# Gated linear attention, then two MLPs: half-chunk score blocks, a state in mid-chunk and four quadrant tiles

## The chip, the cores and the metric

The kernel runs on one core of a Trainium2 chip. The metric is the device time of one execution in microseconds (us); the profile's "span" is the time from the first to the last instruction of the program.

## The reference, cut to what matters

Attention runs over 4 batches, 8 heads, 768 steps, with heads of 48. Its result goes through two MLPs, as 3072 tokens of width 384.

```python
for t in range(S):
    state = alpha[:, :, t, :, None] * state + np.einsum('bhd,bhe->bhde', k[:, :, t], v[:, :, t])
    y[:, :, t] = np.einsum('bhd,bhde->bhe', q[:, :, t], state)
...
h = x @ w_in                               # 384 -> 2048
x = (h * (1.0 / (1.0 + np.exp(-h)))) @ w_out
gate = 1.0 / (1.0 + np.exp(-(x @ w_gate)))     # 384 -> 1536
return (gate * (x @ w_val) @ w_out2)
```

## The kernel before, in words

**Attention in chunks.** The steps are cut into 24 chunks of 128, six to a batch. Heads go in four pairs, one head of a pair on partitions 0 to 47, the other on 64 to 111. For a chunk c, `prep` (L278) runs the decays as two scans on DVE, multiplies the keys by G (DVE) and the queries by A (POOL in the lead, DVE later). `scores` (L310) transposes the keys on TensorE (L319; four, none for a batch's last chunk) and makes keys times queries (L323, 8 matmuls of 48 x 128 by 128 columns). `scores_done` (L331) multiplies the 2 x 4 x 128 columns by the causal mask on DVE (L334), copies the transposed keys out on ACT (L337) and has ACT square both decay tiles (`check`, L273). `results` (L341) adds to one PSUM bank y: masked scores times values (L352, 8 matmuls of 128 columns), and the state times the queries (L373, 8 of 128 columns); between these it makes the chunk's outer products u (L368, 8 matmuls of 48 columns), to which in the lead an identity matmul adds the old state (L364). `state` (L382) makes the next state from u: in the lead one DVE multiply (L389), later an add (L388) and a multiply. A matmul of float32 operands stands in the trace as two records, each with its own weight load.

**Output of attention.** `y_out` (L399) copies y from PSUM into x and x3 on ACT (L406, L407). After each second chunk six DMAs (L412) move rows of x3 into x; x3 has one buffer, x two. `x_out` (L414) splits x into high and low parts (ACT L422, DVE L423), which are the MLP's input.

**Order.** The first LEAD = 9 chunks run before the MLP (loop at L722): in each round `scores` of c+1, the state of the chunk before, `prep` of c+2, `scores_done`, `x_out`, `results` of c, the loads for c+4 and c+5 (SP queue), and from round 3 on one `bit` (L525) of the conversion of the MLP's weights. Weights come as 64-bit floats and are made into a high and a low part by ACT, DVE and POOL; four bits make one pair of weight tiles. Chunks 9 to 23 run inside the first MLP (loop at L796): each item (b, f) is nine matmuls into a hidden tile h (`mm_in`, L575), its activation (`act`, L581), and nine matmuls out (`mm_out`, L598), all of 512 columns through `mm3` (L562). SCORES and RESULTS (L47 to L53) give the items at which a chunk's `scores` and `results` are put into TensorE's program order, so that each chunk interrupts the MLP's matmuls twice; the `prep` of a chunk is put 3 and 2 items ahead of its scores. Up to item 28 each `act` also does half a weight conversion (`half`, L543), from a count `n_half` that the lead leaves behind.

**PSUM.** Of eight banks two are the pool ps_h (h in turn, in the lead also the transposed keys t and u), and two groups of three hold two_banks (scores, later s) and bank (y).

Of the kernel before, what the change touches and what calls it, by code (L numbers as in the profile page):

```python
# [17 lines left out]
P = 128  # L18
# [13 lines left out]
QW = 3 * NP * C  # L32
N = 512
# [17 lines left out]
for _c in range(13, NC):  # L51
    SCORES[_c] = (_c // 4 - 1, (0, 4, 8, 11)[_c % 4], 0)
    RESULTS[_c] = (_c // 4 - 1, (2, 6, 10, 13)[_c % 4], 0)  # L53

# [127 lines left out]
def gated_attention_then_mlps(ctx: ExitStack, tc: tile.TileContext, qka, a0, v, w_in, w_out, w_gate, w_val, w_out2, out):  # L182
# [25 lines left out]
    causal = ap.tile([P, C], F32, name="causal")  # L208

    W = ap.tile([DP, NP * D + 16], F32, name="state")  # L210
    W_all = W[:, : NP * D].rearrange("r (p d) -> r p d", d=D)
# [31 lines left out]
    def constants():  # L243
# [5 lines left out]
        nc.gpsimd.affine_select(out=causal, in_=causal, compare_op=ALU.is_ge, fill=0.0, base=0, pattern=[[1, C]], channel_multiplier=-1)  # L249
# [5 lines left out]
        nc.gpsimd.memset(W, 0.0)  # L255
# [17 lines left out]
    def check(c, i):  # L273

        x = (Gt, At)[i].pop(c)
        nc.scalar.activation(x, x, AF.Square, accum_out=chk[:DP, c, i : i + 1])

    def prep(c, step, p0=0, p1=NP, mul=None):  # L278
# [5 lines left out]
        if step == 0:  # L284
            if p0 == 0:
                Gt[c] = G_at[c % 2]
                At[c] = ap.tile([DP, NP * C], F32, tag="A", name="A", bufs=2)
# [11 lines left out]
        elif step == 1:  # L299
            nc.vector.tensor_tensor_scan(At[c][:, lo:hi], t[:, A_OFF + lo : A_OFF + hi], d1[:, lo:hi], 0.0, op0=ALU.mult, op1=ALU.add)  # L300
        else:
            q = t[:, lo:hi]
            mul.tensor_tensor(q, q, At[c][:, lo:hi], op=ALU.mult)

    S, T, M, KT, U, Y = {}, {}, {}, {}, {}, {}

# [3 lines left out]
    def scores(c, g, apart, p0=0, p1=NP):  # L310

        t = qk[c]
        if p0 == 0:
            S[c] = two_banks(g)
            if not last_of(c):
                T[c] = ps_h.tile([P, N], F32, tag="h", name="t") if apart else bank(g)
        for p in range(p0, p1):
            if not last_of(c):
                nc.tensor.transpose(T[c][:, p * DP : (p + 1) * DP], t[:, NP * C + p * C : NP * C + (p + 1) * C], ident)  # L319
        for p in range(p0, p1):  # L320
            for j in range(2):
                r = 64 * j
                nc.tensor.matmul(  # L323
                    S[c][:, j, p * C : (p + 1) * C],
                    t[r : r + D, NP * C + p * C : NP * C + (p + 1) * C],
                    t[r : r + D, p * C : (p + 1) * C],
                    start=True,
                    stop=True,
                )

    def scores_done(c):  # L331
        for_all = causal.rearrange("s (j i t) -> s j i t", j=1, i=1).to_broadcast([P, 2, NP, C])
        M[c] = ap.tile([P, 2, NP, C], F32, tag="m", name="m", bufs=2)
        nc.vector.tensor_tensor(M[c], S[c].rearrange("s j (i t) -> s j i t", i=NP), for_all, op=ALU.mult)  # L334
        if not last_of(c):
            KT[c] = ap.tile([P, NP, DP], F32, tag="kt", name="kt", bufs=2)
            nc.scalar.activation(KT[c], T.pop(c)[:, : NP * DP].rearrange("t (p d) -> t p d", p=NP), AF.Copy)  # L337
        check(c, 0)
        check(c, 1)

    def results(c, g):  # L341


        y = Y[c] = bank(g)
        first = c % CB == 0

        v_c = vt[c].rearrange("t h e -> t (h e)")
        for p in range(NP):
            for j, n in ((0, 64), (1, D)):
                r, h = 64 * j, (2 * p + j) * D  # L350

                nc.tensor.matmul(  # L352
                    y[r : r + n, p * C : (p + 1) * C], v_c[:, h : h + n], M[c][:, j, p], start=p == 0, stop=first, skip_group_check=True
                )
        s = S.pop(c)
        if not last_of(c):
            u = ps_h.tile([P, N], F32, tag="h", name="u")[:DP] if c < LEAD else s[:DP, 0]
            U[c] = u[:, : NP * D]
            kt = KT.pop(c)
            sums = c < LEAD and not first  # L360
            if sums:
                for j, n in ((0, 64), (1, D)):
                    r = 64 * j
                    nc.tensor.matmul(u[r : r + n, : NP * D], ident[r : r + D, r : r + n], W[r : r + D, : NP * D], start=True, stop=False, skip_group_check=True)  # L364
            for p in range(NP):
                for j, n in ((0, 64), (1, D)):
                    r = 64 * j
                    nc.tensor.matmul(u[r : r + n, p * D : (p + 1) * D], kt[:, p, r : r + n], vt[c][:, 2 * p + j], start=not sums, stop=True, skip_group_check=True)  # L368
        if not first:
            for p in range(NP):  # L370
                for j, n in ((0, 64), (1, D)):
# [527 lines left out]
```

## Time and profile before

| what | value |
|---|---|
| median of 3 runs | 975.56 us (974.47 to 976.59) |
| profiled execution, its own time | 976.87 us |
| its span | 974.8 us |
| mean granted TensorE clock | 0.987 |
| PE, DVE, ACT, POOL busy | 951.3, 450.6, 381.9, 92.9 us |

The program's instructions are listed by line and engine. "PE" is a matmul, "PEld" a weight load, which overlaps matmuls. A duration of a matmul includes its way through the array, so that several overlap; how fast matmuls follow one another is read from their starts.

### The profile page before, as it was taken

What the parts mean: (1) busy time and instruction counts of PE and PEld (TensorE: products, weight loads), DVE (VectorE), ACT (ScalarE), POOL (GpSimd) and SP (SyncE); (2) the same over time, 40 slices, a digit from 0 to 9 for tenths busy, and PEclk for the clock granted to TensorE, in tenths of its full rate; (3) what the DMA queues carried; (4) which work ended last, traced back from release to release, by engine and by line L of the source; (5) the groups of instructions that cost most, each with busy time, mean ns of one, the idle gap of its engine ahead of it and who ended that gap; (6) DMA issues with size and microseconds to landing.
All of it is one profiled execution on the core that took longest, in us unless ns stands there. A gap on an engine that the chain in (4) does not pass through costs nothing.

```text
span 974.8 us, 12868 instructions
## 1 busy us (share of the span) xinstructions
PE 951.3 (98%) x5192; PEld 777.2 (80%) x5192; DVE 450.6 (46%) x640; ACT 381.9 (39%) x707; POOL 92.9 (10%) x105
## 2 busy tenths in 40 slices
PE   7879999999999999999999999999999999999997
PEld 5658887878888888888888888888888888888885
DVE  8777778644543434342766444443232222222221
ACT  3446666443334334333666344433222222221211
POOL 2223323100000000000221111110000000000000
PEclk8899999999999999999999999999999999999999
DMA  9753332130111210003332112001000000000001
GB/s 229 210 150 117 129 100 80 40 107 28 58 42 37 70 38 13 5 1 102 98 98 67 63 65 65 33 1 42 24 1 0 33 1 1 33 1 0 33 1 37
DMA packets 35348, 54.84 MB, mean 56 GB/s; under 512 B 3856, under 2 KB 24368, under 8 KB 35280
## 3 DMA queue, kind: packets, MB, share of 16 engines
q1 hardware_dynamic: 34512, 53.37, 17.9%
q8 instruction: 43, 0.70, 0.3%
q10 hardware_dynamic: 768, 0.56, 0.2%
q14 instruction: 25, 0.20, 0.1%
HBM read 48.02 MB, written 4.72 MB: 54 GB/s over the span
## 4 chain that ended last, share of the span: by engine, by line
PE 89%; DVE 3%; DMA 2%; ACT 2%; issue 1%; POOL 1%; SPq 0%; ACTq 0%; DVEq 0%
PE h L565 13%; PE h L567 13%; PE h L566 13%; PE s L565 6%; PE s L567 5%; PE s L566 5%; PE o L567 3%; PE o L565 3%; PE o L566 3%; PE v L565 3%; PE v L566 3%; PE v L567 3%; PE y L565 3%; PE y L567 3%; PE y L566 3%; PE s L323 2%
## 5 line engine op out<-in xcount | busy, mean ns | idle before, releaser
L565 PE MATMUL h<-x,w 128*128 128x512 f32 x582 | 228.0, 392 | 3.1 <-ACT w L504 1.7
L567 PE MATMUL h<-x,w 128*128 128x512 f32 x582 | 227.0, 390 | 0.8 <-POOL w L522 0.8
L566 PE MATMUL h<-x,w 128*128 128x512 f32 x582 | 227.0, 390 | 0.0
L593 DVE TENSOR_TENSOR gl<-g,gh 128x512 fp32r<-128x512 f32 x168 | 115.9, 690 | 194.9 <-ACT gh L592 194.2
L592 ACT ACTIVATE gh<-g 128x512 fp32r<-128x512 f32 x168 | 106.2, 632 | 157.0 <-DVE g L587 153.9
L565 PEld LDWEIGHTS h<-x,w 128*128 128x128 f32 x582 | 109.2, 188 | 28.0 <-ACT w L504 2.1
L567 PEld LDWEIGHTS h<-x,w 128*128 128x128 f32 x582 | 109.3, 188 | 25.0 <-POOL w L522 1.7
L566 PEld LDWEIGHTS h<-x,w 128*128 128x128 f32 x582 | 109.2, 188 | 22.8
L584 ACT ACTIVATE g<-h 128x512 f32<-128x512 f32 x96 | 57.0, 593 | 154.8 <-PE h L567 154.8
L587 DVE TENSOR_TENSOR g<-v,g 128x512 f32<-128x512 f32 x46 | 31.8, 692 | 178.7 <-PE v L567 178.7
L565 PE MATMUL s<-gl,w 128*128 128x512 f32 x240 | 96.5, 402 | 0.0
L586 ACT ACTIVATE g<-h 128x512 f32<-128x512 f32 x72 | 42.9, 596 | 132.6 <-PE h L567 132.6
L567 PE MATMUL s<-gh,w 128*128 128x512 f32 x240 | 93.7, 390 | 0.0
L566 PE MATMUL s<-gh,w 128*128 128x512 f32 x240 | 93.6, 390 | 0.0
L565 PE MATMUL o<-gl,w 128*128 128x512 f32 x144 | 56.1, 390 | 0.0
L567 PE MATMUL o<-gh,w 128*128 128x512 f32 x144 | 56.1, 390 | 0.0
L566 PE MATMUL o<-gh,w 128*128 128x512 f32 x144 | 56.1, 389 | 0.0
L522 POOL TENSOR_TENSOR w<-tmp,w 128x384 fp32r<-128x384 f32 x36 | 36.4, 1030 | 195.0 <-ACT w L504 195.0
L565 PEld LDWEIGHTS s<-gl,w 128*128 128x128 f32 x240 | 45.0, 187 | 12.4 <-issue 1.4
L587 DVE TENSOR_TENSOR g<-h,g 128x512 f32<-128x512 f32 x26 | 18.0, 692 | 79.3 <-PE h L567 79.3
L565 PE MATMUL v<-x,w 128*128 128x512 f32 x138 | 53.9, 391 | 0.0
L566 PE MATMUL v<-x,w 128*128 128x512 f32 x138 | 53.8, 390 | 0.0
(120 smaller groups left out, 1280.8 us busy)
## 6 DMA issues: line engine op xcount, KB each, us to landing
x<-in_moe_w_in SPq DMA_DIRECT2D x16, 384.0 KB, 3.6
x<-in_moe_w_out SPq DMA_DIRECT2D x16, 384.0 KB, 4.1
x<-in_qka SPq DMA_DIRECT2D x12, 448.0 KB, 4.2
qk<-in_qka SPq DMA_DIRECT2D x11, 448.0 KB, 3.7
v<-in_v SPq DMA_DIRECT2D x24, 192.0 KB, 3.1
raw<-in_moe_w_gate SPq DMA_DIRECT2D x12, 384.0 KB, 3.5
raw<-in_moe_w_val SPq DMA_DIRECT2D x12, 384.0 KB, 3.8
raw<-in_moe_w_out SPq DMA_DIRECT2D x12, 384.0 KB, 3.7
```

The source lines that it names most:

```text
L323: nc.tensor.matmul(S[c][:, j, p * C : (p + 1) * C], t[r : r + D, NP * C + p * C : NP * C + (p + 1) * C], t[r : r + D, p * C : (p + 1) * C] ...
L522: nc.gpsimd.tensor_tensor(l, b[:, i * SW : (i + 1) * SW].bitcast(F32), h.bitcast(F32), op=ALU.subtract)
L565: nc.tensor.matmul(ps, wh, x_l, start=first, stop=False)
L566: nc.tensor.matmul(ps, wh, x_h, start=False, stop=False)
L567: nc.tensor.matmul(ps, wl, x_h, start=False, stop=last)
L584: nc.scalar.activation(g, h, AF.Silu)
L586: nc.scalar.activation(g, h, AF.Sigmoid)
L587: nc.vector.tensor_tensor(g, val, g, op=ALU.mult)
L592: nc.scalar.activation(gh, g, AF.Copy)
L593: nc.vector.tensor_tensor(gl, g, gh.bitcast(F32), op=ALU.subtract)
```

## The change

Each chunk is seen as two halves of 64 steps. Scores are made only inside each half (two diagonal blocks of 64 x 64), and what the second half gets from the first comes through a state taken at mid-chunk. Matmuls of scores, sums (u, now one per half), values and queries become 64 columns wide (sums 48) and lie in the four quadrants of the array; there are 16 of each where there were 8. Keys are transposed for every chunk. W becomes two tiles of two states each. A drain of TensorE stands before the queries. In the MLP there is one visit per chunk: transposes of c+2, sums of c+1, values of c, scores of c+1, queries of c. In the lead the old state is added to u by one identity matmul (`carry`), only for the first half. x3 is gone (x has the fourth block of rows itself), the six DMAs of a pair of chunks go to SP, only those of chunk 7 to both queues. The lead no longer prepares chunk 9; it does 8 conversion bits and one more ACT step in place of 6 bits. The preparations of chunks 9 to 13 have items of their own.

```diff
-CONV = {c: 1 for c in range(3, LEAD)}
+CONV = {c: 1 for c in range(3, LEAD - 1)}
-SCORES = {9: (1, 12, 0), 10: (1, 13, 0), 11: (1, 14, 0), 12: (1, 15, 2)}
-RESULTS = {9: (1, 12, 1), 10: (1, 13, 1), 11: (1, 14, 1), 12: (2, 2, 0)}
-DECAYS = {10: ((1, 9), (1, 10)), 11: ((1, 12), (1, 12)), 12: ((1, 14), (1, 14))}
+FIRST = {"T": (1, 11, 0), "scores": (1, 12, 0)}
+VISIT = {9: (1, 12, 1), 10: (1, 13, 1), 11: (1, 14, 1)}
+G_AT = {9: (1, 5), 10: (1, 7), 11: (1, 9), 12: (1, 11), 13: (1, 13)}
+A_AT = {9: (1, 6), 10: (1, 8), 11: (1, 10), 12: (1, 12)}
+for _c in range(12, NC):
+    VISIT[_c] = (_c // 4 - 1, (2, 6, 10, 13)[_c % 4], 0)
...
+    def scores(c, p0=0, p1=NP):
+        t = qk[c]
+        if p0 == 0:
+            S[c] = bank(0), bank(1) if c < LEAD else ps_h.tile([P, N], F32, tag="h", name="s")
         for p in range(p0, p1):
-            for j in range(2):
-                r = 64 * j
+            for h in range(2):
+                for j in range(2):
+                    r, o = 64 * j, p * C + h * HC
+                    nc.tensor.matmul(
+                        S[c][j][h * HC : (h + 1) * HC, p * HC : (p + 1) * HC],
+                        t[r : r + D, K_OFF + o : K_OFF + o + HC],
+                        t[r : r + D, o : o + HC],
...
     def scores_done(c):
+        for j, s in enumerate(S.pop(c)):
+            nc.vector.tensor_tensor(M[c][:, j], s[:, :UA].rearrange("s (i t) -> s i t", i=NP), for_all, op=ALU.mult)
...
+    def sums(c):
+        for p in range(NP):
+            for h in range(2):
+                for j, n in ((0, 64), (1, D)):
+                    r, o = 64 * j, UA + p * D
+                    if h == 0 or not last_of(c + 1):
+                        nc.tensor.matmul(
+                            yu[r : r + n, h, o : o + D],
+                            kt[h * HC : (h + 1) * HC, p, r : r + n],
+                            vt[c + 1][h * HC : (h + 1) * HC, 2 * p + j],
...
+    def queries(c):
+        nc.tensor.drain()
+        for p in range(NP):
+            for h in range(1 if first_of(c) else 0, 2):
+                for j in range(2):
+                    r, to, n = 64 * j, 64 * (j ^ h), D if h or j else 64
+                    nc.tensor.matmul(
+                        yu[to : to + n, h, p * HC : (p + 1) * HC],
+                        w[r : r + D, h, p * D : p * D + n],
+                        qk[c][r : r + D, p * C + h * HC : p * C + (h + 1) * HC],
...
     def state(c):
+        u = [YU[c - 1][0][:DP, h, UA : UA + NP * D] for h in range(2)]
+        wa, wb = (W[c % 2][:, h, : NP * D] for h in range(2))
+        if c < LEAD:
+            nc.scalar.activation(wb, u[0], AF.Copy)
+        elif first_of(c):
+            nc.vector.tensor_copy(wb, u[0])
         else:
-            nc.vector.tensor_tensor(w, u, w, op=ALU.add)
+            nc.vector.tensor_tensor(wb, u[0], wa, op=ALU.add)
+        if not last_of(c):
+            nc.vector.tensor_tensor(W[(c + 1) % 2][:, 0, : NP * D], u[1], wb, op=ALU.add)
+            if c + 1 in AE:
+                decay(c + 1)
...
+        nc.scalar.activation(x[:DP, :, o, :HC], yu[:DP, 0], AF.Copy)
+        for j in range(2):
+            r, at = 64 * j, 64 * (1 - j)
+            nc.scalar.activation(x[r : r + D, :, o, HC:], yu[at : at + D, 1], AF.Copy)
...
+        def visit(c):
+            open_results(c, 0)
+            if c + 2 < NC:
+                keys(c + 2)
+            if c + 1 < NC:
+                sums(c)
+            values(c)
+            if c + 1 < NC:
+                scores(c + 1)
+                queries(c)
+
+        def visited(c):
+            if c + 5 < NC and c != LEAD - 1:
+                load_decays(c + 5)
...
+            if c == LEAD - 1:
+                for _ in range(3):
+                    way1.bit()
+                way1.a_scalar(2)
+                way1.n_half = 3
+                x_out(c - 1)
```

## Rows read from the trace of the kernel before

**Rows 1.** Page: busy time of each engine; the chain that ended last.

```profile
PE 951.3 (98%) x5192; PEld 777.2 (80%) x5192; DVE 450.6 (46%) x640; ACT 381.9 (39%) x707; POOL 92.9 (10%) x105
...
PE 89%; DVE 3%; DMA 2%; ACT 2%; issue 1%; POOL 1%; SPq 0%; ACTq 0%; DVEq 0%
```

**Rows 2.** Stretches: busy us of PE, PEld, DVE, ACT, POOL; clock, DMA share, GB/s.

```profile
0.00:61.00 61.00, 49.03 (x536) 37.72 (x538) 50.85 (x76) 25.08 (x69) 15.89 (x26) 0.83 0.80 214
61.00:74.00 13.00, 9.05 (x79) 6.23 (x76) 6.46 (x11) 7.09 (x14) 1.31 (x2) 1.00 0.43 129
...
120.00:180.00 60.00, 59.22 (x258) 47.84 (x257) 45.57 (x60) 37.59 (x63) 18.91 (x18) 1.00 0.24 81
```

**Rows 3.** Timeline of PE, one chunk's two visits: start, length (us), line, tiles.

```profile
183.42 0.55 PE L319 MATMUL y<-ident,qk 112*128 112x112 f32 x4
183.90 1.16 PE L323 MATMUL s<-qk 48*128 48x128 f32 x16
184.99 0.50 PE L565 MATMUL s<-gl,w 128*128 128x512 f32 x1
...
186.94 0.40 PE L567 MATMUL y<-gh,w 128*128 128x512 f32 x1
187.27 1.09 PE L352 MATMUL y<-m,v 128*64 128x128 f32 x16
188.18 0.62 PE L368 MATMUL s<-v,kt 128*48 128x48 f32 x16
188.73 1.08 PE L373 MATMUL y<-qk,state 48*64 48x128 f32 x16
189.75 0.50 PE L565 MATMUL h<-x,w 128*128 128x512 f32 x1
```

**Rows 4.** Timeline of PE where only the MLP runs: eleven matmuls, first and last.

```profile
301.74 0.39 PE L566 MATMUL y<-gh,w 128*128 128x512 f32 x1
...
304.00 0.39 PE L567 MATMUL h<-x,w 128*128 128x512 f32 x1
```

**Rows 5.** Groups of PE by form, 304.3 to 306.8 us: busy us, mean ns.

```profile
L352 PE MATMUL y<-m,v 128*64 128x128 f32 x8 | 1.1, 279 | 0.0
...
L368 PE MATMUL s<-v,kt 128*64 128x48 f32 x8 | 0.6, 220 | 0.0
```

**Rows 6.** Timeline of the lead: PE, the transposes of two rounds that follow each other.

```profile
23.02 0.60 PE L319 MATMUL t<-ident,x 112*128 112x112 f32 x4
...
27.74 0.60 PE L319 MATMUL t<-ident,qk 112*128 112x112 f32 x4
```

**Rows 7.** Groups of DVE by form, 6.9 to 61.3 us: busy, mean ns | idle before.

```profile
L334 DVE TENSOR_TENSOR m<-s,causal 128x1024 f32<-128x1024 f32 x9 | 10.8, 1197 | 0.0
...
L423 DVE TENSOR_TENSOR x<-x,x 128x768 fp32r<-128x768 f32 x3 | 3.1, 1028 | 3.5 <-ACT x L422 3.5
L389 DVE TENSOR_TENSOR state<-u,aend 112x192 f32<-112x192 f32 x6 | 2.1, 353 | 1.3 <-PE u L368 0.8 <-POOL x L303 0.3 <-PE y L373 0.2
...
L298 DVE TENSOR_TENSOR qk<-qk,G 112x256 f32<-112x256 f32 x1 | 0.4, 426 | 0.2 <-DMA qk<-in_qka 0.2
```

**Rows 8.** Timeline of DVE late in the lead: three of chunk 9's five preparation steps.

```profile
56.63 1.22 DVE L298 TENSOR_TENSOR qk<-qk,G 112x512 f32<-112x512 f32 x1
57.77 1.21 DVE L300 TENSOR_TENSOR_SCAN A<-qk,d 112x512 f32<-112x512 f32 x1
59.02 0.69 DVE L303 TENSOR_TENSOR qk<-qk,A 112x512 f32<-112x512 f32 x1
```

**Rows 9.** Groups of ACT, 24 to 76 us: the first copy of y_out.

```profile
L406 ACT ACTIVATE x<-y 112x128 f32<-112x128 f32 x7 | 1.9, 278 | 15.4 <-PE y L373 10.0 <-DMA x<-x 5.3
```

**Rows 10.** Waits of PE, longest first: us in total, times, longest.

```profile
PE u L364 <- DVE state L389: 4.8, 2, 4.0
...
PE h L565 <- ACT w L504: 1.7, 1, 1.7
```

**Rows 11.** Line L412, its DMAs on SP: duration ns min/median/max.

```profile
L412 SPq DMA_DIRECT2D x<-x x60: 507/587/1459, 28.9 to 449.1; - x60
```

More of the change, by code (lines that the diff above doesn't have):

```diff
@@ L32 @@
 QW = 3 * NP * C
+HC = C // 2
+UA = NP * HC
 N = 512
@@ L303, in prep, with first_of, open_keys, keys @@
             mul.tensor_tensor(q, q, At[c][:, lo:hi], op=ALU.mult)
-    S, T, M, KT, U, Y = {}, {}, {}, {}, {}, {}
+    S, T, M, KT, YU = {}, {}, {}, {}, {}
     def last_of(c):
         return c % CB == CB - 1
-    def scores(c, g, apart, p0=0, p1=NP):
+    def first_of(c):
+        return c % CB == 0
+    def open_keys(c):
+        T[c] = ps_h.tile([P, N], F32, tag="h", name="t")
+    def keys(c, p0=0, p1=NP):
+        t = qk[c]
+        if c not in T:
+            open_keys(c)
+        for p in range(p0, p1):
+            nc.tensor.transpose(T[c][:, p * DP : (p + 1) * DP], t[:, K_OFF + p * C : K_OFF + (p + 1) * C], ident)
@@ L347, in results, with values @@
+    def values(c):
+        yu, _ = YU[c]
         v_c = vt[c].rearrange("t h e -> t (h e)")
         for p in range(NP):
[L349 to L368, printed above, removed]
@@ L692, in gated_attention_then_mlps @@
         way1.load(0)
-        late = []
-        def states():
-            while late and (last_of(late[0]) or late[0] + 1 in AE):
-                c = late.pop(0)
-                if not last_of(c):
-                    state(c)
-        def results_done(c):
-            late.append(c)
-            if c >= LEAD - 1:
-                states()
+        def visit(c):
[11 more added lines that the diff above has]
+                load_decays(c + 5)
             if c + 4 < NC:
@@ L708, in results_done @@
                 load_values(c + 4)
+        for p0, p1 in ((0, 2), (2, NP)):
+            for s in range(3):
+                prep(0, s, p0, p1, nc.vector)
+            keys(0, p0, p1)
+            scores(0, p0, p1)
+        load_decays(4)
+        keys_done(0)
+        prep(1, 0)
+        keys(1)
+        open_results(-1, 1)
+        sums(-1)
+        scores_done(0)
+        keys_done(1)
+        prep(1, 1)
+        prep(1, 2)
+        state(0)
+        YU.pop(-1)
+        prep(2, 0)
+        early = {}
+        for c in range(LEAD):
+            open_results(c, c % 2)
+            if c + 1 < LEAD:
+                sums(c)
+            values(c)
+            if c + 1 < LEAD:
+                scores(c + 1)
+            else:
+                early[0, 0] = mm_in(ps_h, "h", "in", 0, 0)
+            queries(c)
+            if c + 1 < LEAD:
+                carry(c + 1)
+            if c + 2 < LEAD:
+                keys(c + 2)
+            if c + 2 < LEAD:
+                prep(c + 2, 1)
+                prep(c + 2, 2)
+            if c + 3 < LEAD:
+                prep(c + 3, 0)
+            if c + 1 < LEAD:
+                scores_done(c + 1)
+                state(c + 1)
+            if c + 2 < LEAD:
+                keys_done(c + 2)
+            if c == LEAD - 1:
[4 more added lines that the diff above has]
+                x_out(c - 1)
+            visited(c)
             y_out(c)
@@ L750, in put @@
                 todo.setdefault((i, place), []).append((what, c))
-            for c, (b, f, end) in SCORES.items():
-                put(at[b, f], end, "scores", c)
-                if c > LEAD:
-                    first, then = (at[x] for x in DECAYS[c]) if c in DECAYS else (at[b, f] - 3, at[b, f] - 2)
-                    put(first, 3, "prep0", c)
-                    put(then, 3, "prep1", c)
-            for c, (b, f, end) in RESULTS.items():
-                put(at[b, f], end, "results", c)
-                put(at[b, f] + 1, 1, "x_out", c)
+            b, f, end = FIRST["T"]
+            put(at[b, f], end, "keys", LEAD)
+            b, f, end = FIRST["scores"]
+            put(at[b, f], end, "keys", LEAD + 1)
+            put(at[b, f], end, "first", LEAD)
+            for c, x in G_AT.items():
+                put(at[x], 3, "G", c)
+            for c, x in A_AT.items():
+                put(at[x], 3, "A", c)
+            for c, (b, f, end) in VISIT.items():
+                i = at[b, f]
+                if c > 11:
+                    if c + 1 < NC:
+                        put(i - 3, 3, "A", c + 1)
+                    if c + 2 < NC:
+                        put(i - 2, 3, "G", c + 2)
+                put(i, end, "visit", c)
+                if c + 1 == NC:
+                    put(i, 1, "queries", c)
+                put(i + 1, 1, "x_out", c)
             return todo
```

186 lines of the change are left out of this document (94 added, 92 removed).

## The prediction

> **What bounds the kernel now.** I read the page first. PE is busy 98% of the span and makes 89% of the chain that ended last [rows 1], so the time is mostly a sum over TensorE's instructions. A busy PE is no measure of its pace, so I went on to the busy times by stretch. They show two regimes: in the lead, to 61 us, PE is busy 49 of 61 us and DVE 51, at a mean granted clock of 0.83; from 74 us on PE is all but full while DVE has room (45.6 of 60 us between 120 and 180 us) [rows 2]. The third view is PE's timeline. Where only the MLP runs, eleven matmuls start within 2.26 us, 0.226 us each [rows 4]. A chunk of attention interrupts that twice [rows 3]: from 183.42 to 184.99 us (1.57) for transposes and scores, and from 187.17 (186.94 and one step) to 189.75 us (2.58) for values, sums and queries. After a visit the MLP restarts slowly: from 184.99 to 186.94 us eight steps take 1.95 us in place of 1.81, 0.14 lost. So a usual chunk costs the MLP 1.57 + 2.58 + 2 x 0.14 = 4.43 us.
>
> **The sum is made against** the profiled execution, 976.9 us (span 974.8 and 2.1 around it). The median of the runs is 1.3 us lower, which I take off at the end. A difference of 0.2%, some 2 us, is about what a measurement of this kernel can tell from none.
>
> **Chunks 9 to 23 before.** Fifteen at 4.43 is 66.5. The three that end a batch lack transposes and sums; these take 0.48 and 0.55 us [rows 3], each less a mode change of about 0.1 that stays (187.17 to 187.27), so 3 x 0.84 = 2.5 goes off. The two that begin a batch lack the queries, 2 x 1.02. That leaves 61.9 us.
>
> **Chunks 9 to 23 after.** The unknown is a group of 32 records in four quadrants, which the trace does not have. Its neighbours have 16 records in two tiles. Values, 128 columns, last 1.09 us, of which 0.28 is the last record's way through the array [rows 3, 5]: 0.81 us over 15 steps, 54 ns a record, 108 ns for a pair side by side. Sums, 48 columns: (0.62 - 0.22) / 15 = 27 ns a record, 53 a pair. So two tiles do run at once (the same columns one after the other would need twice the step), and the step falls with the columns. For 64 columns I interpolate: 53 + 16/80 x 55 = 64 ns. Four tiles in the time of two would make a group 8 x 0.064 = 0.51 us, sums as well. Bounds: 8 x 0.053 = 0.42 below; above, tiles that run two by two, 16 x 0.064 = 1.02. I take 0.51, since scores (rows split) and values (columns split) each show their two tiles abreast, and a quadrant is one split on top of the other.
>
> A visit is then: transposes with the mode change 0.48, sums, values and scores 1.53, the drain, queries 0.51, mode change back 0.10, the slower first round of a run twice (187.27 to 188.18 is 0.91 for eight rounds of 0.108, so 0.05 each), restart 0.14. The drain is not in the trace. A mode change, 0.10, is its lower bound; waiting out a matmul (0.28) and filling again (0.22) is 0.50; I take 0.30, as a drain waits for results, which a mode change need not. What is queued behind it on PE is the queries and the next nine MLP matmuls, and nothing else is late for it. Sum: 3.16 us. Thirteen visits (9 to 21) are 41.1; visit 22 has no transposes, 2.8; chunk 23 comes in two small visits, 2.1; the opening of chunks 9 and 10 costs 2.2. That is 48.2 us, **13.7 less** than before. Batch edges save nothing here: with half the records gone, two tiles still do eight rounds each.
>
> What the visits need was made a visit earlier (masked scores, transposed keys, states), some 16 us in the MLP, four to seven in the run of visits 9 to 11. The second scores tile takes the buffer of the h just made, so it waits for that item's activation (0.6 us); transposes, sums and values, 2.5 us, stand before it and hide that. If ACT is in another operation then, 0.1 to 0.3 us of a visit shows. I cost it at nothing.
>
> **The lead.** A round of PE lasts 4.72 us [rows 6]. After, it has transposes 0.48, four groups 2.0, the drain 0.3, mode changes and `carry` some 0.6: about 3.5. But DVE's round stays: two scans 2.42, key product 0.69, mask, state, reciprocal 0.18. The mask goes from one operation of 1.20 to two of 256 elements at 0.43, the state from one of 0.35 to two [rows 7]: 4.84 before, 4.85 after. So an undisturbed round gains nothing; PE's relief is given back to DVE. What does go is chunk 9's preparation, 2 x 1.21 + 1.22 + 0.69 + 0.18 = 4.5 us [rows 8], which moves under the MLP. Its new cover there is DVE at 76% between 120 and 180 us [rows 2]; the weights' conversion, on the same engine, starts half a step ahead (an item, 4 us). If that cover is gone PE waits for weights, up to the 4.5.
>
> Two stalls may shrink. x3 has one buffer, and ACT waited 5.3 us for its DMAs [rows 9]; DVE then waited 3.5 for ACT [rows 7], and PE 4.0 for DVE's state [rows 10]. Now x has two buffers and no x3. The same split still waits for the same DMAs, so what is late next is `x_out` itself. The second weight pair was late by 1.7 us [rows 10]; its bits now come in round 8. Against that: all six DMAs of a pair of chunks are issued by SP, 6 x 0.59 = 3.5 us each second round [rows 11] where half went to ACT, and the loads for c+5 are queued later in the round, behind those of the round before. `y_out` has three copies in place of two, about +0.4 us of ACT, idle half the time. I take **5 us less** in all for the lead: the 4.5, and half a microsecond for both stalls net of the later loads. Bounds: 11 less (all of 4.5 + 4.0 + 1.7 and a little), 3 more (loads that come late).
>
> **Sum.** 976.9 - 13.7 - 5 = 958.2, as a median 957.
>
> **A rule against it.** The Trainium skill, "TensorE: Matmul & The Clock Gate", section "Wait — 56ns, not 53.3ns?", says that matmuls never start less than about 25 ns apart, however few columns they have. The 27 ns a record of the sums would agree with it; but those are two streams, and whether four share such a floor no row here shows. By that floor a group would be an estimated 0.80 us and the sum about 974.
>
> **Rivals.** *Records come one by one.* The densest run in the trace is the 27 ns of the sums [rows 3, 5]. If that is how fast records can follow at all, a group takes 32 x 0.027 = 0.86, not 0.51; over the 60 groups of chunks 9 to 23 that is +21 us, and with the lead's 5 kept the time is 978, near no change. For it: no faster run exists. Against: 48 columns against 128 shows that the step still followed the width. The skill's rule above is this rival's. Chance 0.14.
>
> *Quadrants run two by two* (slower). The place is each group of a visit, the price 1.02 - 0.51 us: 60 x 0.51 = +31, so 988. Then the change doesn't do what it says. It decides from where a group costs 0.51 + 18.7/60 = 0.82 us, 26 ns a record. For it: each of four groups shares both rows and columns of the array with its neighbours, which no row shows. Against: each kind of sharing alone costs nothing. Chance 0.10.
>
> *The lead or the conversion gives back.* Visits as forecast, but late loads or weights take the 5 us and up to 5 more: 962 to 967. For it: DVE's 76% and the lead's DMA share of 0.80 [rows 2]. Chance 0.18.
>
> **The numbers.** The forecast has 0.58, the rest as above. Faster: 0.58 + 0.18 + 0.04 of the first rival, 0.80; the same 0.05; slower 0.10 + 0.05, 0.15. The range 946 to 978 reaches down to a group of 0.45 with the whole of the lead's bound (976.9 - 17 - 11 - 1.3 is 947.6), and up to the first rival; the second is left out.
>
> **What would show it.** Right: one gap in the MLP's matmuls per chunk, about 3 us long, 32 records of values starting within some 0.5 us, first full MLP work at about 69 us in place of 74, DVE and not PE the busiest in the lead, no new wait for weights between 120 and 180 us. Wrong: records 25 ns or more apart in the quadrants; a drain beyond 0.5 us; PE waiting for ACT's h before the scores; SP's loads landing after DVE asks for them; a granted clock that falls in the lead now that PE idles more in each round (it fell before, 0.83).

## The result, and the profile after

The changed kernel takes 981.5 us (median of five runs, 980.5 to 983.6); the kernel before took 975.9 in the same session. The ratio is 1.006, with a 95% interval of 1.0044 to 1.0077. That is 0.6% slower. I had forecast 957 (946 to 978) and a gain. The profiled execution has a span of 979.2 us, 4.4 more than before.

The page of the kernel after, busy time of each engine and the chain that ended last, beside [rows 1]:

```profile
PE 939.0 (96%) x6734; PEld 771.8 (79%) x6734; DVE 453.0 (46%) x689; ACT 399.0 (41%) x744; POOL 100.9 (10%) x107
...
PE 83%; DVE 8%; ACT 4%; issue 3%; DMA 1%; SPq 0%; ACTq 0%; POOL 0%; DVEq 0%; POOLq 0%
```

PE is busy 12.3 us less than before, in a longer span: the work went, and waiting took its place. PE's share of the chain fell from 89 to 83%, DVE's rose from 3 to 8 and ACT's from 2 to 4. The stretches of the kernel after, columns as in [rows 2]; first those of [rows 2], then two parts of the lead:

```profile
0.00:61.00 61.00, 47.61 (x1052) 38.41 (x1053) 48.50 (x85) 30.83 (x83) 22.01 (x27) 0.64 0.75 203
61.00:74.00 13.00, 8.05 (x129) 5.94 (x123) 5.58 (x9) 4.41 (x11) 0.00 (x0) 0.63 0.40 105
120.00:180.00 60.00, 55.62 (x237) 44.99 (x236) 49.04 (x65) 36.63 (x64) 18.73 (x18) 0.97 0.26 86
...
20.00:40.00 20.00, 16.76 (x398) 14.34 (x389) 15.88 (x25) 10.37 (x29) 7.39 (x5) 0.50 0.70 200
40.00:60.00 20.00, 16.65 (x397) 14.26 (x394) 16.10 (x26) 12.63 (x35) 7.11 (x6) 0.50 0.59 152
```

Three things stand here. The granted clock of the lead is 0.50 from 20 to 60 us, the lower of its two levels (1.2 GHz); the mean to 61 us was 0.83 before and is 0.64 now. Between 120 and 180 us, where PE was all but full (59.2 of 60), it now lacks 4.4 us. And from 61 to 74 us every engine is idle a good part of the time; the timelines below show whom they wait for.

The attention inside the MLP did what it should. PE's timeline of the kernel after, a chunk's one visit, beside [rows 3] (the many short lines of values and scores, which overlap, are left out):

```profile
259.39 0.39 PE L630 MATMUL h<-x,w 128*128 128x512 f32 x1
259.63 0.55 PE L328 MATMUL t<-ident,x 112*128 112x112 f32 x4
260.11 0.62 PE L378 MATMUL s<-v,kt 64*64 64x48 f32 x30
...
261.50 0.22 PE L344 MATMUL y<-x 48*64 48x64 f32 x1
261.89 0.67 PE L415 MATMUL s<-qk,state 48*64 48x64 f32 x32 [0.18 <-issue]
262.50 0.50 PE L628 MATMUL s<-gl,w 128*128 128x512 f32 x1
```

From the last matmul to the next are 3.11 us, 2.88 more than a step, where two visits cost 4.15 before. Sums, values and scores, 96 records, start between 260.11 and 261.50: 14.5 ns a record. Read to the nanosecond, the four records of a round of the queries start within 13 to 20 ns, and but for the first the rounds follow one another at some 56 ns. The drain is the step from 261.50 to 261.89.

**Where the time went.** I added up, in both traces, what each interruption of the first MLP costs over its step of 0.227 us.

| place | before | after | difference |
|---|---|---|---|
| visits of chunks 9 to 23, without the restarts behind them | 57.7 | 45.4 | -12.3 |
| lead: first steady matmul, less the steps done by then | 69.3 | 75.5 | +6.2 |
| waits from 140 to 180 us | 1.1 | 5.2 | +4.2 |
| wait ahead of block 2, at 226 us | 0 | 3.5 | +3.5 |

The second line is 74.08 us with 21 steps done before, 77.57 with 9 after. The sum is +1.6; the other 2.8 of the span's +4.4 are smaller ones, and the largest has a cause that the trace shows. Stretches of PE of the kernel after (busy us, clock, DMA share, GB/s), each right behind one of the three long waits, and the timeline at the third:

```profile
77.60:81.30 3.70, 3.70 (x9) 0.50 0.15 34
150.20:153.00 2.80, 2.80 (x7) 0.50 0.00 0
229.40:235.00 5.60, 5.60 (x14) 0.50 0.00 0
...
229.31 0.76 PE L628 MATMUL h<-x,w 128*128 128x512 f32 x1 [3.03 <-DVE x L486]
229.88 0.63 PE L629 MATMUL h<-x,w 128*128 128x512 f32 x1
```

PE was idle, the granted clock behind it was 0.50, and 8, 6 and 12 matmuls started 0.43 us apart in place of 0.227: 5.2 us in all, on top of the waits. Against that, the slow restarts behind the visits, of which there are fewer now, take 2.5 us in place of 4.2. Who keeps PE waiting, the kernel after, beside [rows 10] (us in total, times, longest):

```profile
PE h L628 <- DVE x L486: 11.3, 2, 8.3
...
PE h L628 <- ACT g L647: 3.8, 2, 3.1
```

Three waits make most of it: 8.3 us at the end of the lead and 3.0 at block 2, both for `x_out`'s half on DVE, and 3.1 at 147 us for an activation.

**The end of the lead.** ACT and DVE of the kernel after, two timelines (idle before and its releaser in brackets):

```profile
65.83 1.89 ACTq L475 DMA_DIRECT2D x<-x  x3
67.89 0.85 ACT L485 ACTIVATE x<-x 128x768 fp32r<-128x768 f32 x1 [2.10 <-DMA x<-x]
...
71.38 0.89 ACT L563 ACTIVATE x<-x 128x768 bf16<-128x768 uint16 x1 [1.73 <-DVE x L544]
73.89 0.94 ACT L567 ACTIVATE w<-x 128x384 fp32r<-128x384 f32 x2 [1.62 <-DVE x L578]
...
75.51 0.83 ACT L485 ACTIVATE x<-x 128x768 fp32r<-128x768 f32 x1
```

```profile
68.86 0.96 DVE L486 TENSOR_TENSOR x<-x,x 128x768 fp32r<-128x768 f32 x1 [4.28 <-DMA x<-x]
...
72.31 0.56 DVE L577 TENSOR_TENSOR x<-x 128x768 bf16<-128x768 bf16 x1 [0.43 <-ACT x L563]
72.90 0.96 DVE L578 TENSOR_TENSOR x<-x 128x768 f32<-128x768 f32 x1
76.47 0.96 DVE L486 TENSOR_TENSOR x<-x,x 128x768 fp32r<-128x768 f32 x1 [2.61 <-ACT x L485]
```

The MLP's second item needs `x_out` of chunks 6 and 7 (75.51, 76.47). It stands last in both orders, behind `x_out` of 4 and 5, which itself waited behind three DMA issues on ACT, and behind the pieces (`bit`) of the second weight pair, where ACT and DVE wait for each other by turns. PE had finished the lead's queries at 69.3.

**At 147 us**, DVE and ACT of the kernel after:

```profile
143.82 1.22 DVE L307 TENSOR_TENSOR_SCAN A<-qk,d 112x512 f32<-112x512 f32 x1
145.07 0.69 DVE L310 TENSOR_TENSOR qk<-qk,A 112x512 f32<-112x512 f32 x1
...
146.93 0.96 DVE L578 TENSOR_TENSOR x<-x 128x768 f32<-128x768 f32 x1
```

```profile
147.93 0.94 ACT L567 ACTIVATE w<-x 128x384 fp32r<-128x384 f32 x2 [3.07 <-DVE x L578]
...
149.54 0.58 ACT L647 ACTIVATE g<-h 128x512 f32<-128x512 f32 x1
```

The second half of chunk 9's preparation (1.9 us) holds up the conversion on DVE. ACT's next conversion step is ahead of the next activation in ACT's order, waits 3.07 us, and the activation comes at 149.54; PE has no free h until then.

### The profile page after: what moved, and what is told of

Its sections match the earlier page's. It is cut to its first block, busy times and chain, and to the rows that moved or that the text cites. A ratio compares the mean times of both kernels' runs of the same rounds, so it can differ in the third digit from the quotient of the medians.

```text
span 979.2 us, 16063 instructions
## 1 busy us (share of the span) xinstructions
PE 939.0 (96%) x6734; PEld 771.8 (79%) x6734; DVE 453.0 (46%) x689; ACT 399.0 (41%) x744; POOL 100.9 (10%) x107
## 4 chain that ended last, share of the span: by engine, by line
PE 83%; DVE 8%; ACT 4%; issue 3%; DMA 1%; SPq 0%; ACTq 0%; POOL 0%; DVEq 0%; POOLq 0%
PE h L628 12%; PE h L629 12%; PE h L630 12%; PE s L628 5%; PE s L630 4%; PE s L629 4%; PE o L630 3%; PE o L628 3%; PE o L629 3%; PE v L628 3%; PE v L629 3%; PE v L630 3%; PE y L630 2%; PE y L628 2%; PE y L629 2%
## 5 line engine op out<-in xcount | busy, mean ns | idle before, releaser
L628 PE MATMUL h<-x,w 128*128 128x512 f32 x582 | 231.3, 397 | 16.8 <-DVE x L486 11.3
L629 PE MATMUL h<-x,w 128*128 128x512 f32 x582 | 229.6, 394 | 0.0
L630 PE MATMUL h<-x,w 128*128 128x512 f32 x582 | 229.4, 394 | 0.0
L628 PEld LDWEIGHTS h<-x,w 128*128 128x128 f32 x582 | 111.2, 191 | 42.0 <-issue 12.5
L630 PEld LDWEIGHTS h<-x,w 128*128 128x128 f32 x582 | 110.9, 191 | 24.0
L629 PEld LDWEIGHTS h<-x,w 128*128 128x128 f32 x582 | 111.3, 191 | 23.4
L628 PE MATMUL v<-x,w 128*128 128x512 f32 x138 | 53.9, 391 | 0.0
L629 PE MATMUL v<-x,w 128*128 128x512 f32 x138 | 53.8, 390 | 0.0
L630 PE MATMUL v<-x,w 128*128 128x512 f32 x138 | 53.7, 389 | 0.0
```

What stands on the lines that cost most here:

```text
L628: nc.tensor.matmul(ps, wh, x_l, start=first, stop=False)
L629: nc.tensor.matmul(ps, wh, x_h, start=False, stop=False)
L630: nc.tensor.matmul(ps, wl, x_h, start=False, stop=last)
```

## The experiments

All times are medians; "ratio" is to the kernel before, run on the same chip in the same session. Where none is named, the kernel before took 976.9. The changed kernel was timed in the first session only, where the kernel before took 975.9; in the others that one took up to 977.7, so a difference from 981.5 is good to some 2 us, and the ratios compare better.

**The clock.** Three bfloat16 matmuls of 128 x 512 columns in each round of the lead behind the transposes, eight in the last; nobody reads them.

```diff
+            fill(3 if c < LEAD - 1 else 8)
             if c + 2 < LEAD:
                 prep(c + 2, 1)
```

> The changed kernel with three bf16 matmuls of 112 x 128 by 512 columns added to TensorE's order at the end of each round of the lead (eight at the end of the last one), where TensorE waits for the copy of the transposed keys anyway; their result is not used. Theory A (the clock): the lead got longer because TensorE is granted half its clock from 16 to 67 us, so that its round is 6.4 us of its own work. Full-width work in the wait keeps the clock up: granted clock 0.9 or more between 20 and 60 us, rounds of about 5 us, 8 to 11 us less than the changed kernel (971 to 974). Theory B (DVE and POOL): the round is set by the scans, the mask and POOL's slow query product; then rounds stay at 6.4 us whatever the clock and the time stays at 980 to 984.

979.8 us, ratio 1.0018 (0.9994 to 1.0041). Stretches 20 to 40 and 40 to 60 us, and PE's timeline of this kernel (lines are 6 higher):

```profile
20.00:40.00 20.00, 15.91 (x409) 12.54 (x410) 16.19 (x26) 9.77 (x27) 7.41 (x5) 0.74 0.71 194
40.00:60.00 20.00, 14.74 (x405) 11.04 (x403) 15.70 (x26) 12.40 (x37) 6.39 (x5) 0.83 0.56 161
```

```profile
66.08 0.67 PE L421 MATMUL s<-qk,state 48*64 48x64 f32 x32
66.68 1.90 PE L278 MATMUL fill<-dg 112*128 112x512 bf16 x8
77.47 0.77 PE L634 MATMUL h<-x,w 128*128 128x512 f32 x1 [8.88 <-DVE x L492]
```

The clock rose, the queries came 2.6 us earlier (68.64 to 66.08), and the MLP started when it had before. The lower clock is real, but in the profiled execution what it gives back in the lead goes into the wait for `x_out`. Four rounds, which took 26.1 us in the changed kernel (30.79 to 56.90), took 25.3 here (32.17 to 57.50), far from theory A's 5 us each. That execution took 982.3 us; the median is 1.7 below the changed kernel's, and by the ratios (1.0018 and 1.006, intervals that don't overlap) some 4, so that not all of it is lost.

**The same with narrow work**: pairs of 48 x 64 x 512 matmuls in two quadrants.

> The same filling in the same places, of the same length, but as pairs of narrow matmuls (48 x 64 by 512 columns, in two quadrants of the array at once) in place of full-width ones. Theory A1 (busy time brings the clock): as with the full-width filling, clock 0.9 or more, 971 to 974. Theory A2 (narrow work does not bring it): clock stays near 0.5 between 20 and 60 us, and each of seven rounds gets longer by what the filling takes beyond the wait, 0 to 0.7 us: 981 to 987. Theory B: 980 to 984.

983.8 us, ratio 1.0064 (1.0043 to 1.0086). The granted clock was 0.79 and 0.97 in the two stretches, so matmuls in quadrants raise it too: narrow tiles alone don't hold it down. Four rounds took 22.4 us, and in some of them PE now waits for the masked scores, as in this line of its timeline:

```profile
46.23 0.93 PE L405 MATMUL s<-m,v 64*64 64x64 f32 x29 [2.37 <-DVE m L365]
```

The restart came at 76.1, and the time is no better than the changed kernel's.

**`x_out` of chunks 6 and 7 ahead of the pieces.**

```diff
             if c == LEAD - 1:
+                x_out(c - 1)
                 for _ in range(3):
                     way1.bit()
                 way1.a_scalar(2)
                 way1.n_half = 3
-                x_out(c - 1)
```

> The changed kernel with chunk 7's x_out put ahead of the three conversion bits in the last round of the lead, on ACT and DVE. Theory (order): the MLP's first work on block 1 waited 8.3 us for that split, of which the bits took from 69.7 to 73.9 us on DVE; the MLP goes on at about 72 us in place of 77.6, 4 to 6 us less (975 to 978). Rival: the second weight pair, which the bits make, becomes the next wait, and only 1 to 2 us go.

980.4 us, ratio 1.0033 (1.0011 to 1.0054). PE's timeline of this kernel:

```profile
71.99 0.47 PE L628 MATMUL h<-x,w 128*128 128x512 f32 x1 [1.02 <-DVE x L486]
...
73.89 0.39 PE L630 MATMUL h<-x,w 128*128 128x512 f32 x1
78.75 0.80 PE L628 MATMUL h<-x,w 128*128 128x512 f32 x1 [4.47 <-ACT g L647]
```

Both theories were right in turn: the restart came 5.6 us earlier, and nine matmuls later PE waited 4.5 us, now for the second weight pair's chain ahead of an activation.

**The lead's query product on DVE** in place of POOL.

```diff
-        mul = mul or (nc.gpsimd if c < LEAD else nc.vector)
+        mul = mul or nc.vector
```

> The changed kernel with the lead's query product on DVE in place of POOL. Theory B (contention): POOL's product took 2.05 us (1.27 before) and DVE's key product beside it 1.48 us (0.69 before); with both on DVE the pair costs 1.4 us of DVE in place of 1.5, the scores no longer wait for POOL, rounds get shorter by 0.5 us or more, 4 us or more less than the changed kernel. Theory A (clock): TensorE's round at half clock sets the pace, nothing changes: within 2 us of 981.5.

981.0 us, ratio 1.0042 (1.002 to 1.0065); clock 0.52 and 0.50, rounds of 6.45 us as in the changed kernel, restart 77.8. That POOL and DVE slow each other there is not the cause.

**Chunk 9's preparation back in the lead**, in round 7, where DVE was idle.

```diff
-G_AT = {9: (1, 5), 10: (1, 7), ...}
-A_AT = {9: (1, 6), 10: (1, 8), ...}
+G_AT = {10: (1, 7), ...}
+A_AT = {10: (1, 8), ...}
...
+            if c == LEAD - 2:
+                for s in range(3):
+                    prep(LEAD, s)
+                decay(LEAD)
```

> Undoes one move: chunk 9's preparation and the decay of its state are issued again in the lead, in round 7, where the changed kernel's DVE is idle from 64.6 to 68.9 us (4.3 us; the preparation is 4.5). Theory A, the cover of the moved preparation failed because ACT's conversion step and the next activation stand behind DVE in ACT's order: the stall of 3.31 us at 146.6 us goes (below 0.5), the lead's end moves by 0.3 us at most, and the time is about 3 us less than the changed kernel's, 978. Rival B, DVE's work is conserved, and what goes at 146 comes back: the first steady matmul of the MLP comes 3 to 4.5 us later than 77.6, and the time is the changed kernel's, 980 to 982. Rival C, the stall is the weights' DMA and not DVE's order: the gap at 146 us stays at 3 us.

977.0 us, ratio 1.0008 (0.9988 to 1.0028). ACT's timeline of this kernel, the steps that stood at 147.93 and 149.54:

```profile
144.84 0.94 ACT L567 ACTIVATE w<-x 128x384 fp32r<-128x384 f32 x2 [1.82 <-DVE x L578]
...
146.47 0.58 ACT L647 ACTIVATE g<-h 128x512 f32<-128x512 f32 x1
```

The conversion waits 1.8 us and not 3.1, no wait of PE is left at 147 us, and the lead's restart is at 78.4 (77.6), 0.5 later than A allowed. Otherwise theory A holds: the preparation has no cover there. With the wait the matmuls at half the clock behind it are gone too (granted clock 1.00 from 146 to 150 us), so that more than the 3.3 us of the wait could come back. One of 1.7 us stands at 164 us, where there were 0.8.

**Results copied first in a visit.**

```diff
                     if c + 1 < NC:
+                        y_out(c, False)
                         scores_done(c + 1)
                         state(c + 1)
+                        YU.pop(c)
                         visited(c)
-                        y_out(c)
```

> In a visit, the copies of the results (y_out) are issued ahead of the next chunk's masked scores and state, and ahead of the loads. Theory A, block 2's first matmuls wait at 225.9 us because y_out stands behind the state in ACT's order and its six transfers behind the loads on SP: the wait of 3.2 us there falls to 1 us or less (copies about 0.9 us earlier, transfers about 1 us earlier), the waits of visits 10 and 11 fall as well, and the time is 2 to 3.5 us less, 977 to 979. Rival B, the wait is due to the six transfers alone, one after the other on SP: the wait falls by under 1 us and the time by as little. Rival C: the masked scores now come 1 us later, and PE waits for them at the queries or the next visit; the usual visit grows from 2.87 to over 3.2 us and the time stays or rises.

977.9 us, ratio 1.0016 (0.9994 to 1.0038). PE's timeline ahead of block 2; the bracket was 3.03 in the changed kernel:

```profile
225.01 0.39 PE L630 MATMUL y<-gh,w 128*128 128x512 f32 x1
227.07 0.47 PE L628 MATMUL h<-x,w 128*128 128x512 f32 x1 [1.68 <-DVE x L486]
```

The usual visit stayed at 2.87 (rival C falls), and that of chunk 10 fell from 4.00 to 3.10. The order was half of that wait; in the other half ACT's part of `x_out` still waits 2.39 us for the transfers. Behind this shorter wait the granted clock was 1.00, and the twelve slow matmuls are gone.

**Pieces of the conversion a round earlier**, with `x_out` first (`range(2, LEAD - 1)` for `range(3, LEAD - 1)`, two pieces in the last round).

> The order of the lead's last round: x_out of chunks 6 and 7 ahead of the second weight pair's conversion, as in the run before it, and the conversion's pieces one round earlier (rounds 2 to 7 in place of 3 to 7, two pieces in round 8 in place of three). With x_out moved alone, PE restarted at 72.0 us and then waited 4.6 us at 73.9 us for the second weight pair. Theory A, the end of the lead is a chain of ACT and DVE operations in the order of issue, and the pieces find room earlier: restart at about 72 us, the wait behind it falls from 4.6 to about 2 us (one piece less, 2.0 us on DVE and ACT), and the time is 3 to 5 us below the changed kernel's, 976 to 978. Rival B, the lead's ACT and DVE are full: each of its rounds gets longer, the query step of the last chunk comes 2 us later, and the time is that with x_out alone, 980. Rival C, the clock decides: it stays near 0.5 up to 60 us as before, and so does the time of the lead.

981.3 us, ratio 1.0058 (1.0035 to 1.008): a miss. ACT's timeline of this kernel shows why:

```profile
72.59 0.89 ACT L563 ACTIVATE x<-x 128x768 bf16<-128x768 uint16 x1 [1.89 <-DVE x L544]
73.38 0.83 ACT L485 ACTIVATE x<-x 128x768 fp32r<-128x768 f32 x1
```

The piece that now closes round 7 stands on ACT ahead of `x_out` (73.38) and waits 1.89 us for DVE. The restart was 75.4, and 1.6 us of wait came at 79. None of my three theories had this; it is theory A's rule, which I had applied to one of the two engines' orders.

**The three edits together.**

> The three edits together: x_out first and the weights' pieces a round earlier, chunk 9's preparation in the lead, results copied first in a visit. Theory A, the loss is in the three places and the gain of the attention's steps stands under it: the sum of the single gains, 3 to 5 and 3 and 2 to 3.5, so 9 to 11 us below the changed kernel: 970 to 973, which is faster than the kernel before. Rival B, the places share DVE and ACT, and what one gives the next takes: 975 to 978, with the waits gone where they were and new ones behind the lead's end. Rival C, the lower clock is the loss: the mean granted clock stays below 0.97, and the time at 977 or more.

973.9 us, ratio 0.998 (0.9969 to 0.9991). 7.6 us below the changed kernel, between A's 970 to 973 and B's 975; the restart was still at 76.8 and behind it 1.6 us of wait. Rival C falls: the mean granted clock is 0.961, as low as the changed kernel's 0.962, and the time is lower.

**The lead's end written anew.** Results still come first in a visit; round 8 begins with `x_out` of chunks 6 and 7 and has one piece left. In round 7, from the core of the diff:

```diff
+            if c == LEAD - 2:
+                x_out(c - 2)
+                way1.bit()
+                scores_done(c + 1)
+                y_out(c, False)
+                way1.bit()
+                prep(LEAD, 0)
+                state(c + 1)
+                YU.pop(c)
+                prep(LEAD, 1)
+                prep(LEAD, 2)
```

> The end of the lead written anew, with the results copied first in a visit as in the run before. In round 7: x_out of chunks 4 and 5, a piece of the conversion, the masked scores, the copies of chunk 7's results with their transfers, a second piece, chunk 9's first preparation, the state, the rest of chunk 9's preparation; round 8 begins with x_out of chunks 6 and 7, and has one piece left. Theory A, the order in which ACT and DVE are handed the work sets the restart: in the run with three edits x_out of chunks 6 and 7 stood on ACT behind a conversion step that waited for DVE, and DVE had been idle; now the transfers go out about 2 us earlier, the restart comes at 72 to 73 us in place of 76.8, the wait of 1.6 us behind it goes, and the time is 4 to 6 us below the 973.9 of three edits: 968 to 970. Rival B, DVE has no room: between 61 us and the restart it has some 12 us of work, which is 73.4 us at the earliest; if the pieces wait for one another as before, the restart stays at 76 and the time at 973 to 975. Rival C, transfers behind others: the loads for chunks 11 and 12 come later and a wait shows in the visits of 10 and 11 or at 165 to 175 us, which gives 2 us or more back.

970.9 us, ratio 0.993 (0.991 to 0.9949; 977.7 before): 0.7% faster than the kernel before, and the first run that is clearly faster than both kernels. The restart came at 75.4 with no wait right behind it. It missed the 72 to 73; ACT and DVE of this kernel:

```profile
72.25 0.84 ACT L485 ACTIVATE x<-x 128x768 fp32r<-128x768 f32 x1 [1.30 <-DMA x<-x]
```

```profile
72.48 1.21 DVE L307 TENSOR_TENSOR_SCAN A<-qk,d 112x512 f32<-112x512 f32 x1
73.73 0.69 DVE L310 TENSOR_TENSOR qk<-qk,A 112x512 f32<-112x512 f32 x1
74.34 0.95 DVE L486 TENSOR_TENSOR x<-x,x 128x768 fp32r<-128x768 f32 x1
```

**That scan behind `x_out`** (`prep(LEAD, 1)` and `prep(LEAD, 2)` in round 8, after `way1.a_scalar(2)`).

> The run with the lead's end written anew, with one step moved: the second half of chunk 9's preparation (a scan and a product, 1.9 us of DVE) comes behind x_out of chunks 6 and 7 and not ahead of it. There, ACT's half of x_out ended at 73.1 us, DVE was in the scan until 74.4, and TensorE restarted at 75.4 in place of the 72 to 73 that I expected. Theory A, the restart waits for DVE's half of x_out and for nothing else: it comes at 73.4 to 74.2, 1.2 to 2 us earlier, and the time is 1 to 2 us less, 969 to 970, if the second preparation does not hold up the third weight pair. Rival B, the weights: the third pair's conversion comes behind the preparation, and a wait of 1 us or more appears between 78 and 90 us; the time stays at 971.

971.4 us, ratio 0.994 (0.9925 to 0.9955; 976.7 before): no gain. `x_out`'s two halves now follow each other (73.74, 74.71) and PE's idle time ahead of the restart fell from 3.8 to 2.3 us, as A said; but in this profiled execution the last rounds ran 1.8 us later, and the restart was at 75.8. The waits behind it are 0.3 and 1.9 us at 144 and 162 us (1.3 in the run before). What stays is about equal, and the runs don't tell A from B.

**The bfloat16 matmuls again, on both of these, and in the kernel before.**

> The same, with three bfloat16 matmuls of 512 columns in each round of the lead and eight in the last, whose results nobody reads (they keep TensorE at work where it waits). Alone in the changed kernel they raised the granted clock between 20 and 60 us from 0.50 to 0.74 and 0.83, brought the lead's last attention matmuls 2.6 us earlier and left the restart at 77.5, since that stood behind ACT and DVE. Theory A, with that chain out of the way the clock counts: restart 1 to 2.5 us earlier than without them, and the time as much less. Rival B, the chain still ends last: same restart, same time within 1 us. Rival C, the extra matmuls, some 2 to 3 us of TensorE in all, cost more than the clock gives: up to 2 us more.

967.7 us, ratio 0.9894 (0.9873 to 0.9914), 3.2 below the same without them and the fastest of all; the restart was no earlier (76.2). The profiled executions of the pair took 969.7 and 969.4, so the profiles do not hold the difference of the medians.

> The run before with the bfloat16 matmuls of the earlier runs in the lead (three a round, eight in the last). Theory A, the clock counts once the chain at the lead's end is short: 2 to 3 us less than without them, as the median without this step moved had it (967.7 in place of 970.9), and the first full work of the MLP comes earlier by as much. Rival B, the profiled spans of that pair were 967.6 and 968.0 and the restarts 75.4 and 76.2 us, so the clock gives nothing, and the medians differ by the scatter of the runs: the same time within 1 us, the same restart.

970.2 us, ratio 0.9924 (0.9911 to 0.9937), 1.2 below; restart 75.2.

> A control: the kernel before, with the same bfloat16 matmuls in its lead. Its granted clock was 0.98 between 20 and 40 us and 0.68 between 40 and 60, its DVE is busy there for 14.3 and 19.8 of 20 us, so that the clock does not set its rounds. Theory A, what these matmuls give the changed kernel is a repair of the clock that the change lowered: nothing here, or 0 to 3 us more, as they stand in front of TensorE's own work. Rival B, they would help any form of the lead: 2 us or more less than the kernel before.

979.7 us, ratio 1.0028 (1.0019 to 1.0038): 3.0 slower. In the three forms of the changed kernel these matmuls gave 1.2 to 3.2 us (1.7 in the first, by the medians); in the kernel before, where they raised the granted clock from 0.68 to 0.91 between 40 and 60 us, they cost 3.0. So a higher clock in the lead is not a gain by itself. That they repair something that the change broke would fit, but is not shown: the narrow matmuls raised the clock as much and gave nothing, the intervals of the two later pairs overlap (the first of them barely), and no profiled execution shows where the time goes (this run's took 976.4 us, the shortest of its twelve).

**A second drain** (`nc.tensor.drain()` twice).

> The changed kernel with the drain ahead of the queries issued twice, to measure its price by itself. From the last scores record to the first query there are 0.40 us in a visit of 2.87. Theory A, the price is the emptying of the array, and a second drain finds it empty: the step stays within 0.05 us of 0.40 and the visit of 2.87. Rival B, a fixed price per drain: the step grows by 0.2 us or more, and the visit with it; over some 24 drains up to 5 to 9 us.

PE's timeline of this kernel; the bracket was 0.18 with one:

```profile
262.37 0.22 PE L344 MATMUL y<-x 48*64 48x64 f32 x1
262.85 0.67 PE L416 MATMUL s<-qk,state 48*64 48x64 f32 x32 [0.26 <-issue]
```

The step grew from 0.39 to 0.48 and the usual visit from 2.87 to 2.95. Nearer to A (0.05) than to B (0.2): a drain right behind a drain costs some 0.08, so most of the 0.39 is no fixed price of the instruction. That it is the array running empty and filling again is theory A's reading, which the run fits and does not prove. Its one timed execution took 983.1 us, which says nothing of the difference.

## Why the prediction was wrong

**"Chunks 9 to 23 after" held.** I forecast a group of 0.51 us and got 0.46: four quadrants do run at once, 58 ns for a round of four. The drain was 0.39, inside its bounds of 0.10 to 0.50 and above the 0.30 taken; the two errors partly cancel. A usual visit was 2.88 over the step, 3.02 with its restart, where I had 3.16. Saved were 12.3 us in the visits and 1.8 in the restarts, 14.1, where I had 13.7. The visits of chunks 9 and 10 are 0.7 and 1.1 us longer than the rest; in the second PE waits for ACT's copy of the transposed keys, and such waits I had costed at nothing. Both rivals on the records, one by one (0.86 a group) and two by two (1.02), fall. The Trainium skill, "TensorE: Matmul & The Clock Gate", section "Wait — 56ns, not 53.3ns?", has matmuls start no closer than about 25 ns. The trace has 14.5 ns between records of four quadrants, so it disagrees there; the measurement decides. The Trainium skill, on the same page, section "Measured speedup vs the span model", has the matmuls of a pack run abreast, some 4 ns apart; with that the trace agrees better (four queries within 13 to 20 ns), and I had weighed the other section alone. The trace of the kernel before could have told: its values start in pairs 7 ns apart (187.419 and 187.426 us), the next pair 109 ns behind, which the merged line in [rows 3] hides.

**"The lead" failed**, and it failed by the most: 5 us less was forecast, 3 more was my upper bound, and 6.2 more came. Two sentences of that step were wrong. "An undisturbed round gains nothing" took DVE's 4.85 us as the round, with PE's at 3.5. PE's timeline of the kernel after:

```profile
30.79 0.95 PE L328 MATMUL t<-ident,qk 112*128 112x112 f32 x4
32.43 0.97 PE L378 MATMUL s<-v,kt 64*64 64x48 f32 x29 [0.69 <-ACT kt L332]
...
37.24 0.95 PE L328 MATMUL t<-ident,qk 112*128 112x112 f32 x4
```

A round takes 6.45 us at the granted clock of 0.50, the same without POOL's product: PE's own chain is the round, with transposes of 0.95 in place of 0.55, 0.7 of waiting for the copied keys, and the sums' group 0.97 in place of 0.62. I had named a falling clock as what would show the forecast wrong, and had given it no price. But the rounds are not what the 6.2 us are made of: with the clock raised four of them took 25.3 and 22.4 us in place of 26.1, and the restart still came at 77.5 and 76.1.

The second sentence is "its bits now come in round 8", counted as a gain for the weight pair; it is the step that cost the time. I priced each of the moved operations as busy time, none by its place: three pieces ahead of `x_out` are a chain of ACT and DVE in which each waits for the other, 6.6 us from 68.9 to 75.5, and `x_out`, which releases PE, came behind it. The runs give that place its price: `x_out` first brought the restart from 77.6 to 72.0, 5.6 of the 6.2 us; and only with the pieces, the results and the preparation in an order of their own did the wait not come back as another one (970.9).

**The cover of the moved preparation failed.** I named DVE's 76% as the cover and "half a step ahead" as the conversion's margin, with "up to the 4.5" if it is gone. It was gone: undoing this move alone gave 4.5 us by the medians (981.5 to 977.0), 3.3 of wait and the matmuls at half the clock behind it, which no term of mine had. A share of busy time told nothing of it; the wait passed through ACT's order, conversion step first, activation behind it, to PE. The step should have followed the one that waits for DVE, and asked what is queued behind it.

**A wait ahead of block 2** had no term at all. The visit that I removed as a cost (transposes and scores of chunk 12) stood between the end of block 1's work and `x_out` of block 2; before, DVE's half ended at 213.9 and PE started at once. With that visit gone the same transfers are late. The order inside a visit was half of it, by the run that changes it; that the lost visit is the rest (1.65 us at 212 us in the kernel before, and 1.68 of wait are left) is argued from the traces and was not tried.

The third rival, "the lead or the conversion gives back", named the right places at half their price, 5 to 10 us, and put it down to late loads and weights, where it was the order of ACT and DVE: against the forecast the lead was off by 11.2, the weights at 140 to 180 us by 4.2. With block 2's 3.5 and the 5.2 at half the clock behind the waits, less 0.4 that the visits did better and some 0.6 of smaller differences, that makes 23.1, from the 18.7 less that I had summed to the 4.4 more that the spans show.

## What to carry to other kernels

A change that takes work off the busiest engine is worth what the engines behind it can hand over in time: before pricing a moved step, write down for each in-order engine what stands behind it, and follow that to the bound engine. An operation that takes PE away from its main work can be the cover of a transfer; when it goes, look for what was just in time. When one wait is removed and the time stays, look for what the bound engine waits for next: four single repairs gave 0.2 to 4.5 us here by the medians, and the stage's order written anew, with the others in it, 10.6. And count what a wait of the bound engine costs behind itself: here up to twelve matmuls at half the clock.

## What the runs showed of the hardware that was not expected

Four 64 x 64 tiles of TensorE run at once at some 58 ns for a round of four 64-column float32 records, where two tiles had 108 ns for a pair of 128 columns. The granted clock was 0.91 in the first 20 us of the changed kernel, in which PE waited 2.2 us at a stretch, and then 0.50 for 40 us, in which its longest wait was 1.0 us; a few wide or narrow matmuls in each round brought it to 0.74 to 0.97. Right behind waits of 8.3, 3.1 and 3.0 us it was 0.50 too, for 3 to 6 us in which PE was never idle. A POOL product and a DVE product that run at the same time slow each other: 2.05 and 1.48 us in the lead after, 1.27 and 0.69 where they lie apart before.
